# An attention and channel-mix kernel: w_v loaded in halves, a fused blend, w_k scaled in pieces, and a new instruction order

## The chip, the cores and the metric

The kernel runs on one core of a Trainium2 chip. The time is device time in microseconds (us). Most executions of the kernel before agree within 0.3%. A run more than 1.5% above the fastest of its own kernel is called slow. All traces cited are single executions; their span is some 1.8 us shorter than the time of the same run. A transfer is *issued* when an engine hands it to the DMA queues, and *lands* when its data have arrived.

## The reference

Linear attention for 8 batches of 8 heads, 576 positions of 64 channels, then an RMS norm, then an RWKV channel mix over 512 channels:

```python
kv  = einsum('bhsd,bhse->bhde', k, v)
out = einsum('bhsd,bhde->bhse', q, kv)
x   = out / sqrt(mean(out * out) + 1e-6) * g_norm        # heads side by side: 512 channels
xk  = mu_k * x + (1 - mu_k) * x_prev                     # x_prev: x one position earlier
xr  = mu_r * x + (1 - mu_r) * x_prev
k2  = relu(xk @ w_k) ** 2                                # 512 -> 1024
y   = sigmoid(xr @ w_r) * (k2 @ w_v)                     # 1024 -> 512
```

## The kernel before

The kernel is a list of some 580 named pieces and a hand-searched order of them. Each engine runs its own pieces in list order, so a list entry also fixes the order in which a DMA queue is fed. `kv3.0` is batch 3's k-v product, `qt3` the DMA transpose of its q, `ss5 rr5 ro5 rb5` the sum of squares, reciprocal root, store to and fetch from DRAM of batch 5's scales, `k0`, `r0`, `v0` the products with w_k, w_r and w_v of group 0 (512 rows), `store0.1` the output store of its second half. Nine groups cover the 4608 rows.

```python
def load_w(dst, s, due, land, name):
    def fn(_):
        nc.gpsimd.dma_start(out=dst, in_=s.rearrange("(c p) n -> p c n", p=128))
    return add({"POOL": 0.8}, fn, due=due, land=land, name=name)
# ... cut
p_wv = load_w(w_v_sb, moe_w_v, -698, 5.2, "w_v")        # one transfer
# ... cut: batches 3 to 7 turn q by DMA; the next batch's loads wait for that
def q_turn(_):
    nc.sync.dma_start_transpose(out=get(qT).rearrange("q i (j p) -> q (i j) p", j=NJ),
                                in_=q2.t.rearrange("p i j c -> p (i j c)"))
c = add({"SP": 3.1}, q_turn, deps=parts, ...)
gate = add({"POOL": 0.3}, lambda _: nc.gpsimd.tensor_copy(out=turned, in_=qT.t[0:1, 0, 0:1]), deps=[c], ...)
for n in ("k", "v", "q"):
    whole[(n, b + 1)].deps.append(gate)
# ... cut: batches 5 to 7 send their scales through DRAM
def rms_out(_):
    nc.sync.dma_start(out=get(rd), in_=rc.t[0:128:16, :])
def rms_back(_):
    for e in range(2):
        nc.gpsimd.dma_start(out=get(rs)[64 * e:64 * e + 64],
                          in_=rd.t.rearrange("(i e) c -> e i c", e=2)[e].partition_broadcast(64))
# ... cut: zeros that keep TensorE busy in known gaps ("idle:12" in the order)
def filler(n):
    i = 1 if k_seen[1] < NHP else 0
    for _ in range(n if k_seen[i] < NHP else 0):
        nc.tensor.matmul(get(k_ps[i])[:, 0, 0:128], zero[:, 0:128], zero[:, 128:256], start=not k_seen[i],
                         stop=not k_seen[i])
```

Of the kernel before, what the change touches and what calls it, by code (L numbers as in the profile page):

```python
# [898 lines left out]
```

## Time and profile before

| | before |
|---|---|
| time | 204.55 us median of 3 (204.27 to 204.92; a fourth run came with the result) |
| TensorE busy | 193.6 us of a span of 202.5 |
| VectorE, ScalarE | 147.4, 113.6 us |
| first w_k product, first w_v product | 17.74, 35.88 us in the chain |
| end of TensorE's work | 198.4 us |

The lines themselves are in the prediction below. For the comparison that follows, here are the entries of the two DMA-issuing engines in the kernel before that turned out to matter. First the sync engine's timeline; its columns are the start, how long the issue took, engine, source line, operation, out<-in, and count.

```profile
45.40 1.17 SPq L724 DMA_DIRECT2D out_dram<-out  x2
48.54 4.83 SPq L556 DMA_TRANSPOSE qT<-q  x1
53.43 12.49 SPq L724 DMA_DIRECT2D out_dram<-out  x10
```

One row tile of group 0 is stored (two issues, 256 KB), then batch 3's q is transposed, and only then come the other stores. Next, GpSimd's timeline around batch 7:

```profile
109.75 1.26 POOL L634 DMA_DIRECT2D rs<-rd  x2 [14.94 <-DVE out L821]
110.99 0.18 POOL L562 COPY turned<-qT 1x1 bf16<-1x1 bf16 x1
111.11 0.79 POOL L273 DMA_DIRECT2D q<-in_q_dram  x1
111.90 0.78 POOL L273 DMA_DIRECT2D k<-in_k_dram  x1
112.66 0.78 POOL L273 DMA_DIRECT2D v<-in_v_dram  x1
```

Batch 5's scales are fetched first, the gate opens, then q, k and v of batch 7 go out in 2.3 us. By their time to landing they arrive at 119.5, 122.4 and 125.5.

### The profile page before, as it was taken

Reading aid. Unit: us, or ns where it says so; the run is one execution under the profiler, and the core shown is the slowest. Engines: PE = TensorE matmul, PEld = TensorE weight load, DVE = VectorE, ACT = ScalarE, POOL = GpSimd, SP = SyncE. Lnnn points to the kernel's source line nnn. Section 1 sums busy time; section 2 is a strip of 40 time slices with the busy share of each in tenths; the row PEclk is TensorE's granted clock in tenths of the full one; section 3 lists DMA queues with packets and bytes.
Section 4 is the critical chain, followed back from the end, with each engine's and each line's share of the span. In section 5 each row is a group of like instructions: output and inputs, shape, how many; then the busy total and the mean of one; then the engine's idle time right before and its main releaser. Section 6 shows DMA issues by size and latency. Waiting matters only on the chain.

```text
span 202.5 us, 4076 instructions
## 1 busy us (share of the span) xinstructions
PE 193.6 (96%) x1625; PEld 102.9 (51%) x1645; DVE 147.4 (73%) x324; ACT 113.6 (56%) x145; POOL 32.6 (16%) x52
## 2 busy tenths in 40 slices
PE   7999699999999999999999999999999999999991
PEld 7767484454553444444447744444444444444451
...
DMA  6999999999999999998997999950360117000643
GB/s 166 201 204 204 206 204 206 204 203 227 223 174 189 213 148 128 203 203 191 211 172 151 230 195 196 204 190 3 65 209 2 47 38 228 0 0 0 182 130 107
DMA packets 39800, 31.69 MB, mean 156 GB/s; under 512 B 13636, under 2 KB 34916, under 8 KB 39780
## 3 DMA queue, kind: packets, MB, share of 16 engines
...
q1 hardware_dynamic: 17620, 12.42, 27.0%
q10 hardware_dynamic: 672, 0.89, 1.3%
...
HBM read 35.33 MB, written 9.46 MB: 221 GB/s over the span
## 4 chain that ended last, share of the span: by engine, by line
PE 88%; DVE 4%; DMA 2%; ACT 2%; issue 1%; SPq 0%; DVEq 0%
PE mm L743 28%; PE mm L817 27%; PE mm L795 16%; PE at L520 3%; PE at L599 3%; DMA out<-in_q_dram 2%; PE at L651 2%; PE mm L763 2%; PE at L834 2%; PE mm L834 2%; PE mm L476 2%; PE at L577 1%; ACT uT L184 1%; PE mm L713 1%; PE at L621 1%
## 5 line engine op out<-in xcount | busy, mean ns | idle before, releaser
L743 PE MATMUL mm<-xk,w_k 128*128 128x512 bf16 (+1 forms) x282 | 58.7, 355 | 0.4 <-issue 0.2
L817 PE MATMUL mm<-w_v,sqk 128*128 128x512 bf16 x249 | 57.7, 379 | 0.5 <-issue 0.2
L747 ACT ACTIVATE relu<-mm 128x1024 bf16<-128x1024 f32 x36 | 36.9, 1026 | 35.1 <-PE mm L743 30.7
L743 PEld LDWEIGHTS <-w_k 128*128 128x128 bf16 x288 | 27.3, 98 | 26.1 <-issue 1.6
L817 PEld LDWEIGHTS <-sqk 128*128 128x128 bf16 x256 | 24.5, 98 | 29.1 <-issue 0.9
L795 PE MATMUL mm<-w_r,xr 128*128 128x512 bf16 x137 | 33.7, 380 | 0.4
L750 DVE TENSOR_TENSOR sqk<-relu 128x1024 bf16<-128x1024 bf16 x32 | 21.5, 688 | 12.1 <-ACT relu L747 12.0
L821 DVE TENSOR_TENSOR out<-mm,sig 128x1024 f32<-128x1024 f32 x16 | 19.5, 1221 | 11.7 <-PE mm L817 11.6
L800 ACT ACTIVATE sig<-mm 128x1024 bf16<-128x1024 f32 x18 | 18.3, 1023 | 16.7 <-PE mm L795 16.5
L795 PEld LDWEIGHTS <-xr 128*128 128x128 bf16 x144 | 13.4, 98 | 15.8 <-issue 0.9
L193 ACT ACT_TABLE_LOAD x14 | 18.0, 1283 | 1.4 <-PEq L883 1.2
L693 DVE TENSOR_SCALAR md<-d,cols 128x576 bf16<-128x576 bf16 x56 | 18.1, 365 | 0.3
L184 ACT CAST uT<-at 128x576 bf16<-128x576 f32 x21 | 12.8, 643 | 7.1 <-PE at L599 6.9
L667 DVE TENSOR_TENSOR xT<-uT,rs 128x1152 bf16<-128x1152 bf16 x14 | 10.6, 755 | 5.3 <-ACT rs L655 5.3
L713 PE MATMUL mm<-zero 128*128 128x128 bf16 x131 | 12.2, 257 | 1.1 <-DVE zero L243 1.1
L606 DVE TENSOR_TENSOR sq<-uT 128x576 bf16<-128x576 bf16 x28 | 11.9, 453 | 0.6 <-ACT uT L184 0.3
L655 ACT ACTIVATE rs<-at,eps 128x576 bf16<-128x576 f32 x16 | 11.5, 740 | 0.9 <-PE at L651 0.7
L713 PEld LDWEIGHTS <-zero 128*128 128x128 bf16 x131 | 10.3, 119 | 2.2 <-DVE zero L243 1.1
L634 POOL DMA_DIRECT2D rs<-rd x6 | 3.7, 629 | 45.2 <-DVE md L693 17.5
L696 DVE TENSOR_TENSOR xk<-md,xT 128x1152 bf16<-128x1152 bf16 x14 | 10.6, 759 | 0.5
L696 DVE TENSOR_TENSOR xr<-md,xT 128x1152 bf16<-128x1152 bf16 x14 | 10.6, 758 | 0.5
L679 DVE TENSOR_TENSOR d<-xT 128x1152 bf16<-128x1152 bf16 x14 | 10.6, 755 | 0.3
...
## 6 DMA issues: line engine op xcount, KB each, us to landing
...
v<-in_v_dram POOLq DMA_DIRECT2D x6, 576.0 KB, 12.1
...
```

The costliest lines, as they stand in the source:

```text
L184: nc.scalar.copy(out=dst, in_=src)
L193: nc.scalar.preload_act_table_set(name)
L693: nc.vector.tensor_scalar(out=get(md)[:, hp], in0=d.t[:, hp], scalar1=cols[:, m0 + hp:m0 + hp + 1], scalar2=None, op0=ALU.mult)
L696: nc.vector.tensor_tensor(out=dst[:, hs, c0:c0 + S], in0=md.t[:, hs], in1=xT.t[:, hs, 0:S], op=ALU.add)
L713: nc.tensor.matmul(get(k_ps[i])[:, 0, 0:128], zero[:, 0:128], zero[:, 128:256], start=not k_seen[i], stop=not k_seen[i])
L743: nc.tensor.matmul(get(ps)[:, fc % 2, a0:a1], w_k_sb[:, cc, 128 * fc:128 * fc + 128], xk[:, cc, x0:x0 + a1 - a0], start=(cc == 0), stop=(c ...
L747: nc.scalar.activation(out=get(rt), in_=ps.t, func=AF.Relu)
L750: nc.vector.tensor_mul(out=get(sqk)[:, 2 * f2:2 * f2 + 2, :], in0=rt.t, in1=rt.t)
L795: nc.tensor.matmul(get(ps)[:, ci % 2, :], xr[:, cc, n0:n0 + 128], w_r_sb[:, cc, :], start=(cc == 0), stop=(cc == NHP - 1))
L800: nc.scalar.activation(out=get(sg), in_=ps.t, func=AF.Sigmoid)
L817: nc.tensor.matmul(get(ps)[:, ci % 2, :], sqk.t[:, fc, 128 * ci:128 * ci + 128], w_v_sb[:, fc, :], start=(fc == 0), stop=(fc == NFC - 1))
L821: nc.vector.tensor_mul(out=get(ot)[:, xs, :], in0=ps.t[:, xs, :], in1=sg.t[:, xs, :])
```

## The change

The intent: the first w_v products need not wait for the whole of w_v, the first blends are one VectorE instruction instead of two, the first w_k products need only a quarter of w_k scaled, and a new search of the order is to use this freedom. The whole order list is replaced. The diff of the code (dependency lists that only follow from it are cut):

```diff
-        p_wk.append(scale_w(w_k_sb[:, :, cs], l, None, f"g.w_k{i}", {"DVE": both["DVE"]}))
+        p_wk.append([scale_w(w_k_sb[:, c2:c2 + 2, cs], l, None, f"g.w_k{i}{c2}",
+                             {"DVE": dve_us(1024, 4), "ACT": act_us(1024, True, True)}) for c2 in (0, 2)])
...
-    p_wv = load_w(w_v_sb, moe_w_v, -698, 5.2, "w_v")
+    p_wv = [load_w(w_v_sb[:, 4 * i:4 * i + 4, :], moe_w_v[C * i:C * i + C, :], -698 + 0.1 * i, 2.6, f"w_v{i}")
+            for i in range(2)]
...
+            def fused(_, key, dst, m0):
+                nc.vector.scalar_tensor_tensor(out=dst[:, hp0, c0:c1], in0=d.t[:, hp0, c0:c1],
+                                               scalar=cols[:, m0 + hp0:m0 + hp0 + 1], in1=xT.t[:, hp0, c0:c1],
+                                               op0=ALU.mult, op1=ALU.add)
...
+                if n == 1 and key == "k":
+                    done.append(add({"DVE": dve_us(w) + 0.03}, lambda _, a=(key, dst, m0): fused(_, *a),
+                                    deps=[df, p_cols], bufs=[xT, d], name=f"x{key}0.{hp0}"))
+                    continue
```

The whole order list is replaced. Two places of it (cut to the entries concerned):

```diff
-... store0.0#2 qt3 store0.0 store0.1#2 ... store0.1 gate3 loadq4.0 ...
+... store0.0#2 ... store0.0 ... store0.1#2 store0.1 qt3 gate3 loadq4.0 ...
...
-... r3.2 ss5 r3.3 v3.2.0 ... rr5 ... kv6.0 ... ro5 ... rb5 ... gate6 loadq7.0 ... loadk7.0 loadv7.0 kv7.0 ...
+... v3.2.0 ... gate6 loadq7.0 store3.0 ss5 rr5 ro5 rb5 ... kv6.0 ... loadk7.0 loadv7.0 ... kv7.0 ...
```

More of the change, by code (lines that the diff above doesn't have):

```diff
@@ L15 @@
 ORDER = """
-setup ident loadq0.2 loadk0.2 first_k first_q cast_q:DVE cast_k:DVE first_v table cast_v:DVE idle:61 qtr0.0
-qc0.0#2:ACT idle:2 kv0.0 kvc0.0:ACT qtr0.1 qc0.1#2:ACT loadv0.2 idle:6 kv0.1 kvc0.1:ACT ident9 edge qc0.1:DVE
-qc0.0:DVE idle:1 u0.0 uc0.0:DVE sq0.0 small tr9 u0.1 u0.0#2 uc0.1:ACT sq0.1 cols loadv0.6 loadk0.6 loadq0.4
-uc0.0#2:ACT sq0.0#2 idle:5 ss0.0 rr0.0 mul0.0 idle:3 ss0.1 rr0.1 mul0.1 d0.0 mr0.0:DVE idle:1 ss0.0#2 rr0.0#2
-mul0.0#2 kv0.3 kvc0.3:DVE d0.1 qtr0.2 qc0.2#2:ACT d0.0#2 mk0.0:DVE xk0.0 loadq0.6 qtr0.3 qc0.3#2:ACT qc0.3:ACT
@@ L21 @@
-loadv0.4 qc0.2:ACT loadk0.4 idle:7 kv0.2 idle:4 u0.3 uc0.3:DVE sq0.3 kvc0.2:ACT u0.2#2 uc0.2#2:ACT u0.2 uc0.2:ACT
-sq0.2 idle:13 ss0.3 w_k0 g.w_k0 sq0.2#2 ss0.2 rr0.2 mul0.2 rr0.3 idle:8 ss0.2#2 rr0.2#2 d0.2 mul0.3 loadq1.0 k0.a0.0
-idle:6 qtr1.0 mk0.0#2:ACT qc1.0:ACT mk0.2:DVE mul0.2#2 mr0.1#2:DVE loadk1.0 mk0.1#2:ACT mk0.1:DVE xr0.0 xk0.2
-idle:14 k0.a0.2 loadv1.0 kv1.0 d0.2#2 xk0.1 k0.a0.1 mk0.2#2:DVE kvc1.0:ACT mr0.0#2:ACT u1.00 d0.3 mk0.3#2:DVE
-mk0.3:DVE xk0.3 xk0.2#2 xk0.0#2 xr0.0#2 w_k1 uc1.00:ACT sq1.00 u1.01 uc1.01:ACT sq1.01 g.w_k1 mr0.2:DVE mr0.2#2:DVE
@@ L26 @@
-k0.a0.3 relu0.00 mr0.3:ACT k0.b0 ss1.00 k0.a1.0 relu0.10 mr0.1:DVE ksq0.10 xr0.2 ss1.01 rr1.01 rr1.00 k0.a1.3
-k0.a1.1 k0.a1.2 relu0.01 mr0.3#2:ACT loadq1.4 w_r k0.b1 xr0.1 ksq0.00 xr0.3 loadv1.4 qtr1.2 loadk1.4 kv1.2 g.w_r:DVE
-xr0.2#2 r0.2 relu0.11 qc1.2:DVE kvc1.2:DVE u1.10 uc1.10:ACT r0.3 sig0.1 u1.11 r0.0 r0.1 sig0.0 ksq0.11 ksq0.01
-sq1.10 uc1.11:DVE sq1.11 ss1.11 ss1.10 rr1.10 mul1.0 d1.0 xk1.0 xr1.0 w_v v0.2.0 v0.2.1 v0.3.0 rr1.11 mul1.2 d1.2
-xk1.2 v0.3.1 out0.1 v0.0.0 v0.0.1 v0.1.0 loadk2.0 loadq2.0 qtr2.2 qtr2.0 v0.1.1 qc2.0:DVE out0.0 qc2.2:ACT k1.0
@@ L31 @@
-loadv2.0 kv2.0 kvc2.0:ACT k1.1 relu1.0 xr1.2 loadq3.0 ql3.3:DVE ql3.0:DVE ql3.1:DVE ql3.2:ACT loadk3.0 loadv3.0
-u2.10 uc2.10:DVE sq2.10 u2.01 uc2.01:ACT sq2.01 k1.2 k1.3 k1.4 u2.00 u2.11 store0.0#2 qt3 store0.0 store0.1#2
-relu1.1 uc2.11:DVE uc2.00:ACT sq2.00 ksq1.1 sq2.11 ksq1.0 k1.5 ss2.01 rr2.01 relu1.2 k1.6 ss2.10 rr2.10 store0.1
-gate3 loadq4.0 k1.7 relu1.3 ss2.00 rr2.00 mul2.0 r1.0 r1.1 sig1.0 r1.2 r1.3 ss2.11 sig1.1 loadv4.0 kv3.0 ksq1.2
-ksq1.3 v1.0.0 v1.0.1 v1.1.0 v1.1.1 d2.0 xk2.0 rr2.11 kvc3.0:ACT u3.11 uc3.11:ACT u3.10 uc3.10:ACT v1.2.0 v1.2.1
@@ L36 @@
-u3.01 u3.00 uc3.01:ACT v1.3.0 v1.3.1 mul2.2 d2.2 out1.0 xk2.2 ql4.1:ACT uc3.00:ACT ql4.3:DVE loadk4.0 store1.0#2
-store1.0 ql4.2:DVE ql4.0:DVE qt4 gate4 loadq5.0 out1.1 store1.1 k2.4 k2.5 relu2.2 sq3.00 sq3.10 xr2.2 sq3.01 sq3.11
-ksq2.2 xr2.0 k2.6 k2.7 relu2.3 ksq2.3 k2.2 ss3.10 rr3.10 k2.3 relu2.1 ss3.11 rr3.11 mul3.2 ss3.00 k2.0 rr3.00 d3.2
-k2.1 relu2.0 ss3.01 r2.0 rr3.01 mul3.0 ksq2.0 r2.1 sig2.0 kv4.0 r2.2 r2.3 kvc4.0:DVE ksq2.1 u4.10 u4.01 sig2.1
-uc4.01:ACT uc4.10:ACT v2.0.0 v2.0.1 v2.1.0 xk3.2 d3.0 sq4.01 xk3.0 sq4.10 u4.11 uc4.11:ACT u4.00 ql5.2:DVE
@@ L41 @@
-uc4.00:ACT ql5.1:ACT sq4.11 ql5.3:DVE ql5.0:DVE loadk5.0 loadv5.0 v2.2.0 v2.2.1 v2.1.1 out2.0 ss4.10 rr4.10 v2.3.0
-xr3.0 ss4.01 v2.3.1 out2.1 k3.4 k3.5 ss4.11 rr4.01 relu3.2 xr3.2 ksq3.2 k3.0 rr4.11 mul4.2 sq4.00 d4.2 xk4.2 k3.1
-relu3.0 ksq3.0 qt5 store1.1#2 store2.1#2 k3.6 k3.7 kv5.0 kvc5.0:ACT relu3.3 k3.2 u5.10 uc5.10:DVE u5.11 uc5.11:ACT
-ksq3.3 sq5.11 gate5 loadq6.0 k3.3 relu3.1 ksq3.1 u5.00 uc5.00:ACT sq5.00 u5.01 uc5.01:ACT r3.0 sq5.01 sq5.10 r3.1
-sig3.0 ss4.00 ql6.3:ACT ql6.1:DVE ql6.2:DVE ql6.0:DVE store2.0#2 store2.0 store2.1 v3.0.0 v3.0.1 v3.1.0 v3.1.1
@@ L46 @@
-out3.0 rr4.00 mul4.0 d4.0 xk4.0 r3.2 ss5 r3.3 v3.2.0 v3.2.1 v3.3.0 v3.3.1 rr5 xr4.2 sig3.1 out3.1 xr4.0 loadv6.0
-loadk6.0 kv6.0 k4.6 k4.7 relu4.3 k4.2 k4.3 kvc6.0:DVE qt6 u6.11 uc6.11:ACT ro5 relu4.1 store3.0 store3.0#2 u6.00
-uc6.00:DVE sq6.00 k4.0 u6.01 uc6.01:ACT u6.10 uc6.10:DVE ksq4.3 k4.1 relu4.0 k4.4 k4.5 relu4.2 r4.0 r4.1 sig4.0
-ksq4.1 ksq4.0 sq6.10 sq6.11 sq6.01 ss6 rr6 ro6 rb5 mul5.0 d5.0 gate6 loadq7.0 r4.2 ksq4.2 ql7.0:DVE ql7.3:DVE
-ql7.2:DVE ql7.1:DVE xk5.0 mul5.2 r4.3 sig4.1 v4.2.0 v4.2.1 v4.3.0 v4.3.1 d5.2 xk5.2 out4.1 v4.0.0 v4.0.1 v4.1.0
@@ L51 @@
-v4.1.1 loadk7.0 loadv7.0 kv7.0 out4.0 xr5.2 k5.4 k5.5 relu5.2 k5.6 k5.7 kvc7.0:DVE xr5.0 qt7 u7.10 u7.01 uc7.10:DVE
-uc7.01:ACT ksq5.2 rb6 mul6.2 sq7.10 k5.2 relu5.3 store3.1 store4.1#2 store3.1#2 store4.0 store4.1 u7.00 u7.11
-uc7.11:ACT uc7.00:ACT k5.3 relu5.1 k5.0 sq7.11 k5.1 relu5.0 r5.2 r5.3 sig5.1 r5.0 sq7.01 sq7.00 ss7 r5.1 sig5.0 d6.2
-ksq5.3 ksq5.1 rr7 mul6.0 ksq5.0 v5.2.0 v5.2.1 v5.3.0 v5.3.1 xk6.2 d6.0 xk6.0 k6.2 k6.3 relu6.1 out5.1 ro7 rb7 k6.0
-k6.1 relu6.0 xr6.0 k6.6 k6.7 relu6.3 ksq6.0 ksq6.3 ksq6.1 xr6.2 k6.4 k6.5 relu6.2 ksq6.2 v5.0.0 v5.0.1 v5.1.0 v5.1.1
@@ L56 @@
-out5.0 store5.1#2 store4.0#2 store5.1 r6.2 r6.3 v6.2.0 v6.2.1 sig6.1 v6.3.0 v6.3.1 mul7.2 mul7.0 d7.0 xk7.0 out6.1
-store6.1 d7.2 xr7.2 xk7.2 r6.0 r6.1 v6.0.0 v6.0.1 sig6.0 v6.1.0 v6.1.1 out6.0 store6.0#2 k7.4 k7.5 relu7.2 k8.6 k8.7
-k7.2 k7.3 relu8.3 xr7.0 ksq8.3 ksq7.2 relu7.1 ksq7.1 store5.0#2 store5.0 k7.6 k7.7 relu7.3 ksq7.3 store6.1#2
-store6.0 k7.0 k7.1 relu7.0 k8.0 k8.1 relu8.0 k8.2 k8.3 relu8.1 ksq7.0 r7.2 r7.3 v7.2.0 v7.2.1 ksq8.1 sig7.1 v7.3.0
-v7.3.1 out7.1 r7.0 r7.1 v7.0.0 v7.0.1 v7.1.0 v7.1.1 sig7.0 out7.0 store7.0#2 store7.1 store7.1#2 k8.4 k8.5 relu8.2
@@ L61 @@
-r8.2 r8.3 sig8.1 ksq8.2 ksq8.0 r8.0 r8.1 sig8.0 v8.0.0 v8.0.1 v8.1.0 v8.1.1 store7.0 out8.0 store8.0 out8.0#2
-store8.0#2 v8.2.0 v8.2.1 v8.3.0 out8.1 store8.1 v8.3.1 v8.3.0#2 v8.3.1#2 out8.1#2 store8.1#2 out8.1#3 store8.1#3
+setup ident loadq0.2 first_q first_k cast_k:DVE edge ident9 cast_q:DVE small idle:64 tr9 first_v cast_v:DVE qtr0.0
+qc0.0#2:ACT qc0.0:DVE cols idle:4 kv0.0 qtr0.1 loadk0.2 loadv0.2 idle:1 kv0.1 kvc0.1:DVE kvc0.0:ACT u0.0 qc0.1#2:ACT
+idle:3 u0.0#2 uc0.0#2:DVE sq0.0#2 qc0.1:ACT u0.1 uc0.0:ACT sq0.0 uc0.1:DVE sq0.1 loadv0.4 loadq0.4 loadk0.4 idle:4
@@ new lines @@
+qtr0.2 qc0.2#2:DVE idle:3 kv0.2 table ss0.0#2 idle:2 ss0.0 rr0.0#2 rr0.0 qc0.2:DVE kvc0.2:DVE mul0.0 d0.0 loadq0.6
+idle:6 ss0.1 rr0.1 qtr0.3 qc0.3:DVE loadk0.6 loadv0.6 idle:2 kv0.3 kvc0.3:ACT u0.2 mul0.1 qc0.3#2:DVE xk0.0
+mr0.0:ACT idle:3 u0.3 idle:2 u0.2#2 uc0.2:ACT uc0.3:ACT d0.1 sq0.2 w_k0 idle:7 ss0.2 xk0.1 sq0.3 idle:3 ss0.3
+uc0.2#2:ACT g.w_k00:ACT idle:10 k0.a0.0 rr0.3 mul0.0#2 d0.0#2 mr0.0#2:DVE sq0.2#2 mr0.1#2:DVE mul0.3 d0.3 rr0.2
+k0.a0.1 ss0.2#2 rr0.2#2 w_k1 g.w_k12:ACT mr0.3:ACT mk0.1:ACT g.w_k10:DVE idle:12 k0.a1.0 loadq1.0 k0.a1.1 qtr1.0
@@ new lines @@
+qc1.0:ACT loadv1.0 mul0.2 xk0.3 d0.2 mk0.0:ACT g.w_k02:DVE k0.a0.3 mul0.2#2 xk0.2 d0.2#2 mr0.2:DVE mk0.2:DVE
+mr0.1:DVE k0.a0.2 relu0.00 mk0.3:DVE mr0.3#2:DVE xk0.0#2 loadk1.0 k0.a1.2 k0.a1.3 kv1.0 kvc1.0:ACT u1.00 uc1.00:ACT
+mr0.2#2:ACT u1.01 relu0.01 xk0.2#2 xr0.0#2 k0.b1 relu0.11 ksq0.00 uc1.01:DVE sq1.01 ss1.01 sq1.00 ss1.00 rr1.00
+rr1.01 k0.b0 relu0.10 xr0.1 loadk1.4 w_r xr0.0 xr0.3 xr0.2#2 g.w_r:DVE xr0.2 r0.0 ksq0.11 ksq0.01 mul1.0 loadq1.4
+qtr1.2 qc1.2:DVE loadv1.4 kv1.2 kvc1.2:DVE r0.1 sig0.0 ksq0.10 u1.10 u1.11 r0.2 r0.3 sig0.1 uc1.10:DVE sq1.10 ss1.10
@@ new lines @@
+rr1.10 w_v0 v0.0.0 uc1.11:DVE sq1.11 ss1.11 d1.0 v0.2.0 xk1.0 xr1.0 w_v1 v0.0.1 v0.1.0 v0.1.1 v0.2.1 v0.3.0 rr1.11
+mul1.2 d1.2 xk1.2 out0.0 xr1.2 store0.0#2 loadq2.0 qtr2.0 qc2.0:ACT qtr2.2 v0.3.1 out0.1 qc2.2:DVE k1.2 k1.3 relu1.1
+ksq1.1 loadk2.0 loadv2.0 kv2.0 kvc2.0:ACT loadq3.0 ql3.1:ACT ql3.0:DVE ql3.2:DVE ql3.3:DVE k1.6 k1.7 u2.10
+uc2.10:ACT u2.11 relu1.3 store0.0 k1.0 k1.1 u2.01 uc2.11:DVE uc2.01:DVE sq2.01 u2.00 uc2.00:ACT relu1.0 sq2.00 k1.4
+k1.5 relu1.2 ksq1.2 ss2.01 rr2.01 r1.2 ss2.00 rr2.00 r1.3 sig1.1 r1.0 r1.1 sig1.0 sq2.11 loadk3.0 loadv3.0 kv3.0
@@ new lines @@
+ss2.11 rr2.11 mul2.0 ksq1.3 ksq1.0 v1.0.0 v1.0.1 d2.0 sq2.10 kvc3.0:DVE xk2.0 ss2.10 rr2.10 mul2.2 store0.1#2
+store0.1 qt3 gate3 loadq4.0 v1.1.0 v1.1.1 out1.0 d2.2 xk2.2 u3.11 uc3.11:ACT u3.01 uc3.01:ACT sq3.01 ql4.1:ACT
+ql4.3:ACT ql4.2:DVE ql4.0:DVE v1.2.0 v1.2.1 u3.10 uc3.10:ACT u3.00 v1.3.0 v1.3.1 out1.1 uc3.00:DVE sq3.11 sq3.00
+k2.0 k2.1 ss3.01 rr3.01 relu2.0 k2.2 k2.3 relu2.1 store1.0 ss3.11 ss3.00 rr3.00 rr3.11 k2.6 k2.7 relu2.3 xr2.2 xr2.0
+ksq2.1 ksq2.0 sq3.10 loadk4.0 mul3.0 ksq2.3 k2.4 k2.5 relu2.2 r2.0 ss3.10 loadv4.0 kv4.0 ksq2.2 r2.1 d3.0 xk3.0
@@ new lines @@
+kvc4.0:ACT rr3.10 mul3.2 d3.2 xk3.2 qt4 store1.0#2 v2.0.0 v2.0.1 v2.1.0 v2.1.1 gate4 loadq5.0 sig2.0 out2.0 u4.01
+uc4.01:ACT u4.10 uc4.10:ACT sq4.10 r2.2 loadv5.0 loadk5.0 ql5.2:DVE r2.3 sig2.1 ql5.0:DVE ql5.1:DVE ql5.3:ACT qt5
+store1.1#2 k3.6 u4.11 uc4.11:DVE u4.00 k3.7 uc4.00:DVE relu3.3 store2.0#2 gate5 xr3.2 sq4.00 k3.0 k3.1 relu3.0
+ss4.10 sq4.01 rr4.10 k3.4 k3.5 xr3.0 ss4.01 rr4.01 relu3.2 v2.2.0 v2.2.1 ksq3.3 ss4.00 sq4.11 store1.1 ss4.11 v2.3.0
+v2.3.1 out2.1 store2.1#2 rr4.11 mul4.2 ksq3.2 rr4.00 d4.2 r3.2 r3.3 sig3.1 k3.2 kv5.0 kvc5.0:DVE xk4.2 ksq3.0 k3.3
@@ new lines @@
+relu3.1 ksq3.1 store2.0 u5.01 uc5.01:ACT sq5.01 xr4.2 u5.10 uc5.10:ACT loadq6.0 ql6.3:DVE ql6.1:DVE ql6.0:DVE
+loadv6.0 loadk6.0 r3.0 r3.1 u5.11 uc5.11:ACT u5.00 uc5.00:ACT mul4.0 sq5.00 ql6.2:ACT qt6 v3.0.0 v3.0.1 v3.1.0
+v3.1.1 sig3.0 v3.2.0 v3.2.1 v3.3.0 v3.3.1 sq5.10 d4.0 xk4.0 sq5.11 out3.0 store3.0#2 gate6 loadq7.0 store3.0 ss5 rr5
+ro5 rb5 out3.1 store2.1 kv6.0 kvc6.0:DVE k4.4 k4.5 relu4.2 ksq4.2 xr4.0 k4.6 k4.7 relu4.3 k4.2 u6.01 uc6.01:ACT
+u6.11 uc6.11:DVE k4.3 relu4.1 k4.0 k4.1 u6.00 ksq4.1 uc6.00:DVE u6.10 sq6.11 uc6.10:ACT sq6.10 sq6.00 relu4.0 sq6.01
@@ new lines @@
+r4.2 r4.3 sig4.1 ksq4.3 ql7.3:DVE ksq4.0 ql7.0:ACT ql7.1:DVE ql7.2:ACT mul5.0 mul5.2 d5.0 d5.2 xk5.0 xk5.2 store3.1
+r4.0 ss6 r4.1 v4.0.0 sig4.0 v4.0.1 v4.1.0 v4.2.0 v4.2.1 v4.3.0 v4.1.1 out4.0 v4.3.1 out4.1 loadk7.0 loadv7.0 xr5.2
+qt7 store3.1#2 kv7.0 kvc7.0:DVE rr6 ro6 k5.4 k5.5 relu5.2 k5.2 k5.3 relu5.1 store4.0 store4.1#2 store4.0#2 xr5.0
+u7.00 u7.11 ksq5.2 uc7.00:DVE uc7.11:ACT sq7.11 k5.6 k5.7 relu5.3 sq7.00 ksq5.3 ksq5.1 k5.0 k5.1 relu5.0 ksq5.0 rb6
+mul6.0 mul6.2 u7.10 uc7.10:ACT u7.01 uc7.01:ACT d6.2 sq7.01 sq7.10 r5.0 r5.1 v5.0.0 v5.0.1 v5.1.0 v5.1.1 sig5.0
@@ new lines @@
+out5.0 ss7 rr7 ro7 r5.2 r5.3 v5.2.0 v5.2.1 v5.3.0 v5.3.1 sig5.1 d6.0 xk6.2 xk6.0 k6.6 out5.1 store5.1 store5.0 k6.7
+relu6.3 ksq6.3 k6.2 k6.3 relu6.1 k6.0 k6.1 relu6.0 k6.4 k6.5 relu6.2 rb7 xr6.2 xr6.0 r6.0 r6.1 ksq6.0 sig6.0 ksq6.1
+mul7.0 ksq6.2 store5.1#2 store5.0#2 store4.1 mul7.2 d7.0 d7.2 xk7.0 xk7.2 r6.2 r6.3 sig6.1 v6.2.0 v6.2.1 v6.3.0
+v6.3.1 out6.1 v6.0.0 v6.0.1 v6.1.0 v6.1.1 out6.0 store6.0#2 store6.1#2 store6.0 store6.1 k7.2 k7.3 relu7.1 k8.2 k8.3
+relu8.1 k7.6 k7.7 relu7.3 xr7.0 ksq7.1 xr7.2 ksq7.3 ksq8.1 k7.4 k7.5 relu7.2 k7.0 k7.1 relu7.0 ksq7.0 ksq7.2 k8.4
@@ L63 @@
+k8.5 relu8.2 k8.6 k8.7 relu8.3 k8.0 k8.1 relu8.0 ksq8.0 r7.2 r7.3 sig7.1 ksq8.3 r7.0 r7.1 v7.0.0 v7.0.1 v7.1.0
+sig7.0 v7.1.1 v7.2.0 v7.2.1 v7.3.0 v7.3.1 out7.0 store7.0#2 ksq8.2 out7.1 store7.1#2 store7.0 r8.2 r8.3 sig8.1 r8.0
+r8.1 sig8.0 v8.0.0 v8.0.1 out8.0 store8.0 v8.2.0 v8.2.1 out8.1 store8.1 v8.1.0 v8.1.1 v8.3.0 v8.3.1 v8.3.0#2
+v8.3.1#2 store7.1 out8.0#2 store8.0#2 out8.1#2 store8.1#2 out8.1#3 store8.1#3
 """.split()
@@ L479, in k_part @@
                                          stop=(k_seen[i] == NHP and fc % 2 == 1))
-                k_parts[i].append(add({"PE": 0.44}, k_part, deps=[ka, p_wk[i]], bufs=[k_ps[i]], mode="full",
+                k_parts[i].append(add({"PE": 0.44}, k_part, deps=[ka, p_wk[i][hp // 2]], bufs=[k_ps[i]], mode="full",
                                       due=T0 + 0.44 * (hp + NHP * i), name=f"k0.a{i}.{hp}"))
@@ L771, in mix @@
                     m = k_parts[i] if half == 0 else [add(
-                        {"PE": 1.75}, k_half, deps=need["k"] + [p_wk[i]], bufs=[ps], due=u, mode="full", name=f"k0.b{i}")]
+                        {"PE": 1.75}, k_half, deps=need["k"] + p_wk[i], bufs=[ps], due=u, mode="full", name=f"k0.b{i}")]
                     k_all += m
@@ L782, in mix @@
                 ms.append(add({"PE": 0.865}, lambda _, fc=2 * f2 + x, ps=ps: k_mm(_, fc, ps),
-                              deps=ms or need["k"] + [p_wk[f2 // 2]], bufs=[ps, sqk], due=u + x, mode="full",
+                              deps=ms or need["k"] + p_wk[f2 // 2], bufs=[ps, sqk], due=u + x, mode="full",
                               name=f"k{g}.{2 * f2 + x}"))
@@ L836, in mix @@
                             ms.append(add({"PE": 0.865 * (cs[1] - cs[0]) / C}, v_last,
-                                          deps=ms[-1:] or sqs + [p_wv, sg_done.deps[0]], bufs=[ps, sqk, ot],
+                                          deps=(ms[-1:] or sqs + [sg_done.deps[0]]) + [p_wv[part_]], bufs=[ps, sqk, ot],
                                           due=u + 2 * x + part_, mode="full", name=f"v{g}.{2 * c2 + x}.{part_}"))
@@ L851, in mix @@
                                   lambda _, ci=2 * c2 + x, part_=part_, ps=ps: v_mm(_, ci, part_, ps),
-                                  deps=ms[-1:] or sqs + [p_wv, sg_done.deps[0]], bufs=[ps, sqk, ot],
+                                  deps=(ms[-1:] or sqs + [sg_done.deps[0]]) + [p_wv[part_]], bufs=[ps, sqk, ot],
                                   due=u + 2 * x + part_, mode="full", name=f"v{g}.{2 * c2 + x}.{part_}"))
```

## The prediction

> **What bounds the kernel now.** I first read the page's busy table and slices, to see which engine is full and where it is not.
>
> ```profile
> PE 193.6 (96%) x1625; PEld 102.9 (51%) x1645; DVE 147.4 (73%) x324; ACT 113.6 (56%) x145; POOL 32.6 (16%) x52
> PE   7999699999999999999999999999999999999991
> DMA  6999999999999999998997999950360117000643
> ```
>
> TensorE is full from the third slice to the last but one. But "busy" counts filler: at L713 the kernel multiplies zeros to fill gaps, 131 times. So next I read the stretches between landmarks of the chain (columns: stretch, its length, PE, PEld, DVE, ACT, POOL busy, clock, DMA share, GB/s).
>
> ```profile
> 17.74:35.88 18.14, 16.52 (x221) 11.69 (x220) 15.51 (x46) 14.01 (x21) 5.53 (x7) 1.00 1.27 205
> 35.88:58.18 22.30, 21.88 (x245) 11.20 (x248) 18.70 (x39) 15.29 (x19) 2.66 (x4) 1.00 1.24 214
> 160.35:182.79 22.44, 22.34 (x103) 10.17 (x104) 10.81 (x18) 9.21 (x9) 0.00 (x0) 1.00 0.24 71
> 198.40:202.50 4.10, 0.00 (x0) 0.00 (x0) 0.75 (x2) 0.00 (x0) 0.00 (x0) 0.84 0.47 130
> ```
>
> From 35.88 us to 198.40 TensorE idles 1.3 us in all (0.42 in the first of these rows, about 0.1 in each of the others). No order of the same matmuls can win more than that there. The room is in the head, before 35.88, which the chain of work that ended last shows in order of time (start, us, what).
>
> ```profile
> 17.74 0.44 PE mm L476 x4
> 18.18 0.34 PE mm L713 x6
> ...
> 19.14 0.89 PE mm L713 x14
> ...
> 22.06 1.18 ACT uT L184 x2
> 23.24 0.94 ACT relu L747
> 24.18 0.04 issue
> 24.22 1.91 PE mm L763 x16
> ...
> 35.88 4.96 PE mm L817 x23
> ```
>
> The first real w_k product starts at 17.74, and the first w_v product at 35.88. Between them the chain leaves TensorE for two uT copies and a relu on ScalarE (22.06 to 24.22, less the end of the last matmul: about 1.5 us idle) and spends 0.34 + 0.89 us on fillers. So about 2.8 us can be won after 17.74, and more only if 17.74 itself moves.
>
> The second limit of the head is the load stream. From the timeline, with each transfer's issue-to-landing time:
>
> ```profile
> 8.14 0.79 POOL L304 DMA_DIRECT2D w_k<-in_moe_w_k_dram  x1
> 10.88 0.80 POOL L304 DMA_DIRECT2D w_k<-in_moe_w_k_dram  x1
> 12.29 0.81 POOL L304 DMA_DIRECT2D w_r<-in_moe_w_r_dram  x1
> 17.85 0.89 POOL L304 DMA_DIRECT2D w_v<-in_moe_w_v_dram  x1 [0.52 <-DMA q<-in_q_dram]
> ```
>
> With 8.0, 12.1, 14.7 and 17.2 us to landing, they land at 16.1, 23.0, 27.0 and 35.05. From 27.0 to 35.05 the stream brings w_v (1024 KB) and two half batches (288 KB each): 1600 KB in 8.05 us, 199 KB per us. It works off transfers in issue order, so a landing is a sum of sizes. w_v, whole, lands 0.8 us before its first use: the first v piece could not have come earlier than 35.05 however fast the rest was.
>
> **What the skill says.** (1) "VectorE: DVE Perf Modes", section "The perf-mode tier table": tensor_scalar in bf16 reaches 4x, tensor_tensor 2x; scalar_tensor_tensor, which the fused xk is, has no row. The trace agrees on large tiles: 128x2048 tensor_scalar 748 ns (w_r), 128x1152 tensor_tensor 755 ns. The fused form's speed no run shows yet. (2) "DMA: Bandwidth & Descriptors", "Issuing engines are not separate DMA queues": transfers of all engines share 16 engines and interleave. The slices agree: about 200 GB/s throughout the head. (3) "ScalarE: Activation LUTs", "What ACT_TABLE_LOAD costs": about 1283 ns each; the trace has 14 of mean 1283 ns. (4) "TensorE: Matmul & The Clock Gate", "What's actually happening": a cold array runs at half clock. The first 61 fillers took 6.21 us, 102 ns each; six later ones 0.34 us, 57 ns each. So I price later fillers at 57 ns.
>
> **The change, part by part.**
> *w_v in halves.* One more issue on POOL (0.8 us, off the path). The first 512 KB lands 512/199 = 2.6 us sooner, at 32.5; the second at 35.05. The new order puts v0.0.0 and v0.2.0 (0.86 us each) before the first use of the second half, so v may start at 33.3 with no wait. This allows up to 35.88 - 33.3 = 2.6 us; it gives only what the rest of the head delivers.
>
> *xk fused for 256 columns, four times.* It removes a tensor_scalar and a tensor_tensor. Their mean durations are 311 and 291 ns, but back to back each costs about 0.20 us (successive starts 19.51, 19.71, 19.91). One operation at one element per cycle would be (an estimate, from the 0.96 GHz that the same page states) 256/960 = 0.27 us plus 0.07: 0.34. Saved: 4 x (0.40 - 0.34), about 0.2 us of VectorE, and one md less before each xk.
>
> *w_k scaled in four.* VectorE had 2 x 2048 columns (0.66 and about 0.95 us by successive starts). It keeps two pieces of 1024 (about 0.35 each) and ScalarE takes two, about 1.1 us each: 256 and 320 columns took 519 and 560 ns, 0.64 ns per column, so 1024 take about 1.0. That frees 0.9 us on VectorE and adds 2.1 to ScalarE. The first product no longer waits for a scale of all four head pairs.
>
> *Order.* w_k's second half is now issued before batch 1's loads and lands at 16.1 + 2.6 = 18.7 instead of 23.0, so its products can fill the hole at 22.06. Fillers fall from 131 to 126. VectorE up to the second group-0 output takes on more copies (two more 576-column uT casts, 0.8 each; more qT), net about +1.2 us; it has 1.8 us idle near 24 to 27 and more near 9 to pay with. ScalarE gets one more table load (15): its first copy brings one load, the rsqrt set is loaded after it; by my walk it has 0.4 us spare. The later transposes of q move ahead of output stores, and the gated loads with them: slack, not time.
>
> *The head walked by hand* with the durations above. The q cast is now behind the k cast and ident9, so v's cast ends near 8.15 instead of 7.93 and kv0.0 starts 0.4 late; but the first u no longer waits for a second qT copy (about 9.5 instead of 9.77). First rsqrt near 12.5 instead of 11.6. ScalarE scales w_k's first piece from about 16.35 to 17.4, so k0.a0.0 starts near 17.5, only 0.3 sooner. Then: twelve fillers to 19.3, a1.0 and a1.1 to 20.25, qtr1.0 to 20.8, a0.3, a0.2, a1.2, a1.3 to 22.6, a wait for batch 1's k (16.1 + 2.6 + 2.6 + 3 x 1.45 = 23.1 by the stream) and kv1.0 to 23.7, relu and kv copy to 24.1, u1 to 24.55, b1 to 26.3, ss1 and b0 to 28.55, r0.0 and qtr1.2 to 30.0, kv1.2, r0.1, u1 to 31.85, r0.2, r0.3, ss1.10 to 33.85. So v0 starts at 33.85 with the same work done but one ss1.11 (0.25): 35.88 - 33.85 - 0.25 = 1.8 us won, if no handover costs anything. The walk counts few semaphore delays over some forty hops, so I take 1.4 of it.
>
> After v0: kv2.0 needs batch 2's v, landed at 43.7 before; by the walk kv2.0 starts at 43.9, just behind it. The relay of batch 3's q waits for its landing at 46.7 as before. I take 0.1 us of net loss in the 162 us that follow. Sum: 204.55 - 1.4 + 0.1 = 203.2, rounded down a little for the looser gates.
>
> **Rivals.**
> *A: the load stream decides.* The bytes before batch 2's v and batch 3's q are the same, so their landings cannot move, and an early store of group 0 would even delay them. For: the DMA row is at 9 tenths throughout the head. Against: the walk shows these two just met. Then TensorE waits near kv2.0 and gain shrinks to 0 to 0.7: 203.9 to 204.5.
> *B: VectorE becomes the bound between 28 and 48.* It runs without a gap there before and has 1.2 us more to do. Then relu, sqk and out come late and mm buffers hold TensorE: 203.8 to 205.
> *C: the head gains all and the later waits go too:* 1.8 + the w_v cap's remainder 0.7 + part of the 1.3 us: 201.5 to 202.
> *D: the q relays, earlier in program order for batch 6, block VectorE or ScalarE until q lands.* Before, q6 landed at 100.9, 8.4 us after issue. Costs 0.5 to 1.5 us near 92 to 98.
>
> **Range and chances.** Half way between the walk and its losses: 203.1 us, with 201.7 to 204.6 holding C's better half and most of A, B, D. More than 2% faster means below 200.5, which needs over 4 us: more than the holes of the head and all later idle together (2.8 + 1.3) unless 17.74 moves by far; 0.03. Slower by 2% needs 4 us of new waits: 0.02.
>
> **What would show it.** Right: first w_k product within 0.5 us of 17.5; no ScalarE step in the chain near 22 to 24; w_v halves landing near 32.5 and 35; first w_v product near 34; TensorE idle after it still 1 to 2 us. Fused xk near 0.34 us by successive starts. Wrong: a DMA wait before kv1.0 or kv2.0 over 0.5 us, sqk or out releases of TensorE (B), TensorE gaps behind q relays near 92 to 98 (D), or a first w_k product later than 18.2.

## More of the kernel before

The two facts that matter later: the sync engine (SP) issues output stores, q transposes and the scale stores in one sequence, and GpSimd (POOL) issues all casting loads and the scale fetches in another. An entry that waits holds up everything behind it in its sequence (the fetch that waits 6.72 us in the profile after is an example).

## The result and the profile after

| | before | after |
|---|---|---|
| time, median (range) | 204.43 us (204.27 to 204.92, 4 runs) | 211.38 us (209.71 to 212.83, 4 runs) |
| ratio of fast runs | | 1.0333, interval 1.0255 to 1.0412 |
| mean granted TensorE clock | 0.997 (profiled run) | 0.980 to 0.988 |

All these runs are fast ones. The ratios here and below compare the fast runs of the two kernels; they are not quite the ratios of the medians. The kernel became 3.3% slower. The profiled run of the changed kernel is the slowest of its four (212.83 us).

The page after, with TensorE's busy share, its slices, its clock and the DMA share:

```profile
PE 195.6 (93%) x1618; PEld 103.6 (49%) x1640; DVE 148.3 (70%) x325; ACT 115.3 (55%) x143; POOL 33.0 (16%) x53
PE   7999899999499999999999992899999999999992
PEclk9999999999999999999999999589999999999999
DMA  6999999999949969989999799930057006000445
```

There are two new dents in TensorE's row, one in the eleventh slice (about 53 to 58 us) and one in the twenty-fifth (about 127 to 132), and behind the second the clock row falls to 5. TensorE's timeline names what ended these two gaps (in brackets the idle time and its releaser), and shows that the head did what was hoped:

```profile
33.97 1.03 PE L828 MATMUL mm<-w_v,sqk 128*128 128x512 bf16 x4
...
58.07 0.95 PE L531 MATMUL at<-v,k 96*64 96x64 bf16 x48 [2.73 <-DMA v<-in_v_dram]
...
132.39 1.49 PE L531 MATMUL at<-v,k 96*64 96x64 bf16 x48 [4.30 <-DMA v<-in_v_dram]
```

The first w_v product starts at 33.97 (the timeline of the kernel before has it at 35.71). But batch 3's k-v product waits 2.73 us for v and batch 7's waits 4.30 us. The stretches around the second wait (start and end, length, PE, PEld, DVE, ACT, POOL busy, clock, DMA share, GB/s):

```profile
55.34:58.07 2.73, 0.00 (x2) 0.03 (x2) 1.58 (x3) 2.71 (x3) 0.00 (x0) 1.00 1.31 103
128.09:132.39 4.30, 0.00 (x1) 0.03 (x2) 3.32 (x5) 0.00 (x0) 0.00 (x0) 0.94 1.25 88
132.39:139.84 7.45, 7.23 (x67) 3.51 (x71) 2.43 (x5) 1.02 (x1) 1.26 (x2) 0.58 0.93 251
139.84:206.90 67.06, 66.73 (x330) 30.63 (x336) 38.16 (x67) 29.73 (x30) 1.23 (x2) 1.00 0.24 67
```

After the second wait the clock is at 0.58 for 7.45 us, which alone costs about 7.45 x 0.42 = 3.1 us. The starts agree: from batch 7's k-v product to the end of TensorE's work it is 74.50 us here and 71.55 before, so 2.95 us more for the same work. After the first, shorter wait the clock stays at 1.00.

Why the loads were late is in the two issuing engines. The sync engine after:

```profile
42.16 4.31 SPq L735 DMA_DIRECT2D out_dram<-out  x8
48.19 6.91 SPq L567 DMA_TRANSPOSE qT<-q  x1
```

All four row tiles of group 0 (eight issues, 1 MB) now go out before batch 3's transpose, in the middle of the loads of batch 3's k and v. Those landed at 49.5 and 53.3 before; they land at 53.7 and 57.9 now, and their last part shares the DMA engines with the transpose (as the old kernel's v did). And GpSimd after, around batch 7:

```profile
109.68 0.77 POOL L273 DMA_DIRECT2D q<-in_q_dram  x1 [0.39 <-DVE kv L186]
117.17 1.26 POOL L645 DMA_DIRECT2D rs<-rd  x2 [6.72 <-DMA rd<-rc]
118.53 0.79 POOL L273 DMA_DIRECT2D k<-in_k_dram  x1
119.31 0.78 POOL L273 DMA_DIRECT2D v<-in_v_dram  x1
```

The fetch of batch 5's scales stands between q's load and those of k and v, and waits 6.72 us for the scales to arrive in DRAM. So k and v are issued at 118.5 and 119.3 instead of 111.9 and 112.7, and v lands at 132.3 instead of 125.5.

TensorE's own clock of progress (starts in the timelines, us) sums it up:

| | before | after | after, behind (+) or ahead (-) |
|---|---|---|---|
| first w_v product | 35.71 | 33.97 | -1.7 (one ss of 0.25 still to do: -1.5) |
| batch 3's k-v product | 57.24 | 58.07 | +0.8 (two ss of 0.25 each still to do: +1.3) |
| batch 7's k-v product | 126.80 | 132.39 | +5.6 |
| end of TensorE's work | 198.35 | 206.89 | +8.5 |

(`ss` is a sum of squares; the new order puts some behind the product.) The parts add up: -1.5 + 2.73 + 4.30 + 2.95 for the lowered clock is 8.5. The medians differ by less, 7.0 us, since the profiled run is the slowest.

### The profile page after: what moved, and what is told of

Read it like the earlier page. It is cut to its first block, busy times and chain, and to the rows that moved or that the text cites. A ratio compares the mean times of both kernels' runs of the same rounds, so it can differ in the third digit from the quotient of the medians.

```text
span 211.1 us, 4070 instructions
## 1 busy us (share of the span) xinstructions
PE 195.6 (93%) x1618; PEld 103.6 (49%) x1640; DVE 148.3 (70%) x325; ACT 115.3 (55%) x143; POOL 33.0 (16%) x53
## 4 chain that ended last, share of the span: by engine, by line
PE 63%; DMA 27%; POOL 6%; issue 2%; DVE 1%; ACT 0%; DVEq 0%; ACTq 0%
PE mm L754 22%; PE mm L828 20%; DMA v<-in_v_dram 19%; PE mm L806 10%; DMA k<-in_k_dram 5%; PE at L531 3%; DMA rd<-rc 3%; POOL q L273 2%; PE mm L774 2%; POOL k L273 2%; PE at L845 2%; PE mm L845 2%; PE at L610 2%; PE at L662 1%; POOL v L273 1%
## 5 line engine op out<-in xcount | busy, mean ns | idle before, releaser
L754 PE MATMUL mm<-xk,w_k 128*128 128x512 bf16 (+1 forms) x281 | 60.0, 364 | 0.6 <-issue 0.4
L754 PEld LDWEIGHTS <-w_k 128*128 128x128 bf16 x288 | 28.1, 100 | 28.0 <-issue 4.3
L806 PE MATMUL mm<-w_r,xr 128*128 128x512 bf16 x135 | 33.0, 380 | 0.6 <-issue 0.3
L531 PE MATMUL at<-v,k 96*64 96x64 bf16 x336 | 7.4, 203 | 7.5 <-DMA v<-in_v_dram 7.0
L184 ACT CAST uT<-at 128x576 bf16<-128x576 f32 x17 | 10.3, 640 | 4.7 <-PE at L610 4.4
L724 PE MATMUL mm<-zero 128*128 128x128 bf16 x126 | 11.7, 251 | 1.1 <-DVE eps L244 1.1
L531 PEld LDWEIGHTS <-k 96*64 96x64 bf16 x336 | 6.6, 118 | 10.1 <-issue 9.4
L573 POOL COPY turned<-qT 1x1 bf16<-1x1 bf16 x4 | 0.7, 176 | 67.2 <-DMA qT<-q 67.2
```

Of the source, the lines that this page charges most:

```text
L531: nc.tensor.matmul(get(ps)[64 * r:64 * r + 64, 0, c:c + HD], kin.t[:, 2 * hp + e, HD * j:HD * j + HD], vin.t[:, 2 * hp + e, HD * j:HD * j ...
L754: nc.tensor.matmul(get(ps)[:, fc % 2, a0:a1], w_k_sb[:, cc, 128 * fc:128 * fc + 128], xk[:, cc, x0:x0 + a1 - a0], start=(cc == 0), stop=(c ...
L806: nc.tensor.matmul(get(ps)[:, ci % 2, :], xr[:, cc, n0:n0 + 128], w_r_sb[:, cc, :], start=(cc == 0), stop=(cc == NHP - 1))
```

## The experiments

**Theory Q**: the order in which the two issuing engines feed the DMA queues costs the time, at two places, and the second wait costs again through the clock. **Rival W**: the new parts and the copies moved to VectorE and ScalarE cost it.

### e6_old_order: the parts without the new order

The change's code, with the order list of before (w_v0 w_v1 for w_v, four scalings on VectorE for two, no separate md, the product of mu and the difference, for the fused columns).

> The parts of the change (w_v in halves, fused xk, w_k scaled in four pieces, all four on VectorE) in the order of the kernel before. Theory Q (the loss lies in the new order): the same as the kernel before within 0.6 us, 203.8 to 205 us. Rival W (the parts cost): 206 us or more.

Measured: 204.22 us median (204.03 to 205.51, 20 runs), ratio 0.9988, interval 0.9975 to 1.0001. The parts alone cost nothing and win nothing; the first w_v product starts at 36.24. The loss lies in the order. W falls as far as it blames the parts; the copies that it also blames are part of the new order, and e4 and e7 bear on them.

### e4_head_only: the new head, then the old order

All the parts and the new order up to `out0.1`, then the old order for all pieces that are left.

> All parts of the change and its order up to the second output of group 0, then the order of the kernel before for all that is left. Theory Q: the head's 1.9 us are kept and none of the new waits comes, 202.3 to 203.5 us. Rival W (what the new head moves to VectorE and ScalarE is given back later): 204.5 or more.

Measured: 203.91 us (203.49 to 204.52, 4 runs), ratio 0.9979, interval 0.9956 to 1.0002. So the new head does no harm later, but 202.3 to 203.5 was expected: 0.5 us by the medians is all that stays, and the interval reaches no gain at all. The first w_v product starts at 34.15, and then:

```profile
44.09 0.95 PE L530 MATMUL at<-v,k 96*64 96x64 bf16 x48 [0.51 <-DMA v<-in_v_dram]
```

TensorE, being ahead, runs into batch 2's v, which lands at 43.9 here and landed at 43.7 before. It starts batch 3's k-v product 0.5 us before the old kernel (56.70 to 57.24), batch 6's also 0.5 (106.37 to 106.91), and ends 0.7 us before it (197.69 to 198.35). What is lost of the lead is lost before batch 3's product; the old order keeps the rest. This is the prediction's rival A, with its wait near `kv2.0` and its 203.9 to 204.5 us.

### e1_kv7_loads: batch 7's k and v ahead of the scale fetch

```diff
-loadq7.0 store3.0 ss5 rr5 ro5 rb5 ... loadk7.0 loadv7.0 xr5.2 qt7
+loadq7.0 loadk7.0 loadv7.0 store3.0 ss5 rr5 ro5 rb5 ... xr5.2 qt7
```

> The changed kernel, with the loads of batch 7's k and v moved ahead of the store and fetch of batch 5's scales on GpSimd, directly behind the load of batch 7's q. Theory Q (queue order costs the time): the two loads are issued near 111 us instead of 118.5, v of batch 7 lands before about 126, TensorE no longer waits 4.3 us for it near 128 and its clock is not lowered after it (2.7 us more), so 5 to 7 us less than the changed kernel: 204.5 to 206.5 us. Rival W (the extra work of the new parts and of the moved copies on VectorE and ScalarE is what costs): nothing changes, 210 to 212.

Measured: 212.71 us (212.03 to 214.13, 4 runs), ratio 1.0416. My expectation missed. Batch 7's v lands at 124.6 and its product no longer waits, but:

```profile
127.20 0.95 PE L530 MATMUL at<-v,k 96*64 96x64 bf16 x48
133.91 0.58 PE L753 MATMUL mm<-xk,w_k 128*128 128x512 bf16 x1 [5.77 <-DVE out L831]
```

The next product waits 5.77 us for VectorE to empty a PSUM buffer (the memory that TensorE's products go to). VectorE's timeline says what held that up:

```profile
126.92 0.76 DVE L677 TENSOR_TENSOR xT<-uT,rs 128x1152 bf16<-128x1152 bf16 x1 [6.67 <-DMA rs<-rd]
...
132.65 2.35 DVE L831 TENSOR_TENSOR out<-mm,sig 128x1024 f32<-128x1024 f32 x2
```

VectorE stood 6.67 us before batch 5's scales, whose two halves now landed behind k and v at 125.6 and 126.8 instead of 121.0 and 121.9, and the outputs stand behind that multiplication in its order. Putting one transfer first only exchanged the waiting engine. The place of `rb5` in GpSimd's sequence was a symptom; the scales themselves come too late.

### e2_qt3_first: the transpose ahead of the stores

```diff
-ql3.3:DVE ... store0.0 ... store0.1#2 store0.1 qt3 gate3
+ql3.3:DVE qt3 ... store0.0 ... store0.1#2 store0.1 gate3
```

> The changed kernel, with the transpose of batch 3's q put ahead of three of group 0's four stores on the sync queue, as the kernel before had it. Theory Q: k and v of batch 3 land near 49.5 and 53.5 instead of 53.7 and 58.0, the 2.7 us wait of TensorE at 55.4 goes. The stores now delay batch 4's loads instead, which have some slack. The second wait, near 128, stays in part: 1 to 3 us less than the changed kernel, 208.5 to 210.5 us. Rival W: no change.

Measured: 202.87, 204.65, 208.13 and 208.21 us, all below the range expected. Two of these count as slow, so the ratio of the fast runs, 0.9969 (0.9916 to 1.0022), rests on two runs and says little. The trace is of a slow run, 208.21; the two fast ones left none, so whether they wait at batch 7 too is not known. What it shows of batch 3 is clear: v lands at 53.5, its product starts at 56.07 without a wait (before 57.24, after 58.07). Batch 7's still waits 2.89 us in this run. In the two long runs the mean clock is 0.990 and 0.982, in the two short ones 1.000 and 0.999. In the profiled one it is 0.70 and 0.87 in the two 4 us stretches after the wait (some 1.7 us lost). The first collision is shown, with its cause.

### e3_both: both moves

The edits of the two runs before, together.

> The changed kernel with both moves of the two runs before. Theory Q: both waits gone, the 1.9 us won in the head stay: 202.3 to 204 us, faster than the kernel before by 0.4 to 2 us. Rival W: 209 to 211.

Measured: 210.72 us (209.89 to 212.02, 4 runs), ratio 1.0317. Also a miss, for the reason of e1: batch 3's product starts at 55.60 without a wait, but a w_k product waits 5.13 us at 131.62 for the output behind batch 5's scales.

### e5_warm_wait: keeping TensorE busy in the wait

```diff
             def kv_mm(_, hps=hps, hp0=hp0, ps=ps):
+                for _i in range(70 if b == 7 else 0):
+                    nc.tensor.matmul(get(ps)[:, 0, 0:128], zero[:, 0:128], zero[:, 128:256], start=True, stop=True)
```

> The changed kernel with 70 more products of zeros (about 4 us at 57 ns each) just ahead of batch 7's k-v product, so that TensorE is kept busy in most of the wait for batch 7's v. Theory C (the wait costs twice: 4.3 us itself, and some 2.7 us because the clock is lowered after it): the wait stays, the granted clock stays at 0.99 or more, 2 to 3.5 us less than the changed kernel, 208 to 209.5 us. Rival: the lower clock has another cause than the idle time, the records show it again and the time is 211 or more.

Measured: 209.00 us (208.34 to 210.01, 4 runs), ratio 1.0228, mean clock 0.998 to 1.000, against 211.38 with 0.980 to 0.988 for the changed kernel: 2.4 us less by the medians, from work that computes nothing. The wait is still there, filled:

```profile
126.88 4.07 PE L527 MATMUL at<-zero 128*128 128x128 bf16 x70
131.07 0.95 PE L532 MATMUL at<-v,k 96*64 96x64 bf16 x48
```

```profile
131.07:138.50 7.43, 7.38 (x84) 3.67 (x85) 4.19 (x9) 3.20 (x4) 1.26 (x2) 1.00 0.96 245
```

In the same 7.4 us after batch 7's v the clock is 1.00, not 0.58. From batch 7's product to the end of TensorE's work it is 71.56 us, as in the kernel before (71.55) and not the 74.50 of the changed kernel. So the second wait is paid for twice, and the second payment, 2.9 us, is the clock's.

### e7_qt3_norm5 and e8_norm5: batch 5's scales early

Theory Q2: the scales come late because the new order puts `ss5` behind all of group 3's w_v products and its store (`ro5`) behind two output stores on the sync engine. In e8 this alone is undone, with `rb5` ahead of batch 7's loads again; in e7 the transpose move of e2 is added.

```diff
-sig3.0 v3.2.0 v3.2.1 v3.3.0 v3.3.1 sq5.10 d4.0 xk4.0 sq5.11 out3.0 store3.0#2 gate6 loadq7.0 store3.0 ss5 rr5 ro5 rb5
+sig3.0 sq5.10 sq5.11 ss5 rr5 ro5 v3.2.0 v3.2.1 v3.3.0 v3.3.1 d4.0 xk4.0 out3.0 store3.0#2 rb5 gate6 loadq7.0 store3.0
```

> Only the second of the two moves: batch 5's scales early, group 0's stores still ahead of batch 3's transpose. Theory Q2: the 2.7 us wait for batch 3's v near 55 stays, the one near 128 goes with its lowered clock: 204.8 to 206.5 us. If the first collision alone carried on into the second one: 208 or more.

> The changed kernel with the transpose of batch 3's q ahead of group 0's stores, and with batch 5's sum of squares, rsqrt, store and fetch of its scales moved before the second half of group 3's w_v products, so that the scales are fetched before batch 7's q, k and v, as in the kernel before. Theory Q2 (the new order brings batch 5's scales too late, so that their fetch and batch 7's loads collide, whichever goes first): the fetch is issued near 108 instead of 115 to 117, v of batch 7 lands before 125, no wait over 0.5 us at batch 7's k-v product nor for the group-4 output, clock 0.99 or more, 202.3 to 203.6 us. Rival (the transfers of this stretch are too many for any order of theirs): a wait of 2 us or more stays near 125 to 132, 205 us or more.

Measured, e8: 206.43 us (205.54 to 207.79, 4 runs), ratio 1.0112, as expected: the scales are fetched at 108.9, v of batch 7 lands at 125.8, there is no wait at batch 7's product and the clock of the profiled run is 0.998. At batch 3's product TensorE still stands 1.72 us; the profile puts that wait down to a sigmoid, but v of batch 3 lands at 56.9 and the product starts at 57.02.

Measured, e7: 204.51 us (203.57 to 205.56, 14 runs), ratio 0.9999, interval 0.9977 to 1.0020. Both collisions are gone, and with them the whole loss of 7 us. The products of batches 3 and 7 start without a wait:

```profile
56.42 0.95 PE L530 MATMUL at<-v,k 96*64 96x64 bf16 x48
...
127.94 0.95 PE L530 MATMUL at<-v,k 96*64 96x64 bf16 x48
```

So Q2 holds. But 204.5 is the time of the kernel before, not the 202.3 to 203.6 that I expected: part of that miss is the next run.

### e7b_again: a second look at e7

> The kernel with both moves once more, for a second profile: the first one showed a 1.7 us wait for the scaling of w_k's second half near 19 to 20.6, which landed late. If that is jitter of the load stream, this profile has a wait of 0.5 us or less there and ends near 203.6 us; if the wait belongs to this order, it is there again and the time is 204.5 or more.

Measured: 204.09 us, one run. In the first profile of e7 the second half of w_k's scaling had come late and TensorE waited 1.71 us for it at 20.62; here there is no such wait, and the first w_v product starts at 33.69. So that wait is not in every execution, and the new head has no slack against it. But the time is 204.09 and not 203.6. TensorE is 2.0 us ahead of the old kernel at batch 3's k-v product (55.20; 1.5 if the two ss still to do are counted), 1.0 at batch 6's (105.91 to 106.91), 0.3 at batch 7's (126.49 to 126.80) and at the end (198.05). The first loss is the repair's own. With the same TensorE work, batch 5's product to batch 6's is 11.79 us in the changed kernel and 12.41 here: `ss5`, moved forward, now waits between its eight small matmuls for VectorE's squares and takes 0.88 us to the next piece instead of 0.36. The second loss is this:

```profile
119.48 7.08 PE L827 MATMUL mm<-w_v,sqk 128*128 128x512 bf16 x31 [0.66 <-DVE sqk L760]
```

VectorE's timeline has, just ahead of that squaring, a copy of batch 7's q that waited 0.84 us for its load:

```profile
118.40 0.42 DVE L185 COPY q<-q 96x384 bf16<-96x384 bf16 x2 [0.84 <-DMA q<-in_q_dram]
118.74 0.68 DVE L760 TENSOR_TENSOR sqk<-relu 128x1024 bf16<-128x1024 bf16 x1
```

This is the prediction's rival D, at batch 7 instead of batch 6.

### e9_before_stores: one of the collisions alone, in the kernel before

```diff
-store0.0#2 qt3 store0.0 store0.1#2 ... store0.1 gate3
+store0.0#2 store0.0 store0.1#2 ... store0.1 qt3 gate3
```

> The kernel before with one thing alone from the new order: all four stores of group 0 ahead of batch 3's transpose on the sync queue. Theory Q: k and v of batch 3 land some 4 us later, v near 57.5, a little after TensorE wants it at 57.2, and all gated loads after it move by as much: 204.8 to 206.5 us. If nothing is lost (204.2 to 204.7), the stores cost the changed kernel only because it was ahead there.

Measured: 205.08 us (204.26 to 210.38, 20 runs, one of them slow), ratio 1.0037, interval 1.0017 to 1.0058. The total fits, the place does not. In the profiled run (206.38 us) v of batch 3 lands at 55.1, in time for 57.84. The delay is passed from gate to gate (batch 4's q is issued at 59.1 instead of 56.0) and comes out at batch 6:

```profile
109.18 0.95 PE L520 MATMUL at<-v,k 96*64 96x64 bf16 x48 [1.27 <-DMA k<-in_k_dram]
```

So the stores cost the old kernel 0.8 us by the medians; most of the 2.73 us in the changed kernel came because its v landed 2.8 us later still and TensorE was ahead. Its stores also went out earlier (from 42.2, here from 46.0) and delayed k as well (53.7, here 49.5).

### e10_head_kv2: e4 with batch 2's product one piece later

e4 with `kv2.0` behind `k1.1` instead of ahead of it, so that batch 2's v is there.

> The hybrid of the new head and the old remainder, with batch 2's k-v product put one piece (k1.1, 0.86 us) later, since TensorE stood 0.5 us before it waiting for v of batch 2. If the load stream caps the head's gain only at this product: 0.3 to 0.5 us less than the hybrid, 203.3 to 203.7 us, the best of all. If the gain is given back elsewhere: 203.8 to 204.3.

Measured: 203.91 us (203.47 to 204.06, 6 runs), ratio 0.9966, interval 0.9938 to 0.9994: the only interval that lies wholly below the kernel before, by a third of a per cent. But the median is that of e4, 203.91, so the move itself is not shown to win anything. The wait for v is gone and batch 2's product starts at 44.43, but TensorE then waits 0.47 us, until 45.85, for the copy of that product instead: the time is in the range that was expected if the gain is given back elsewhere.

## Why the prediction was wrong

**What bounds the kernel, and the head: right.** The first w_k product started at 17.25 (17.5 in the walk), batch 1's k-v product waited for k until 23.08 (23.1), the halves of w_v landed at 32.4 and 34.9 (32.5 and 35.05), and v began at 33.97 (33.85). As a start time the walk was closer than the discount that I gave it. But its 1.8 us were counted from the chain's 35.88; from the timeline's 35.71 the gain measured is 1.5. One reading was careless: TensorE's row is not full from the third slice on, its fifth is at 6 tenths, which is the hole that the chain then shows at 22 to 24 us.

**The parts: small and partly mis-sized.** The fused blend takes 478 ns alone and 0.40 us by successive starts (19.12 to 19.52 in e7b), not 0.34, so it saves nothing against two operations of 0.20. A w_k piece on ScalarE takes 1142 ns (1.0 to 1.1 was estimated). Neither e6 (all four w_k pieces on VectorE) nor e4 (two on ScalarE) shows a loss from it.

**The step that failed** is "The later transposes of q move ahead of output stores, and the gated loads with them: slack, not time", with its sum, "I take 0.1 us of net loss in the 162 us that follow". I compared TensorE's and VectorE's orders of the two kernels carefully and the issuing engines' hardly. Batch 3's transpose moved behind three more row tiles of stores, and batch 5's scales moved into the middle of batch 7's loads; both were in the orders that I had. In place of 0.1 us the runs show 2.73 us of wait at batch 3, 4.30 us at batch 7 and 2.95 us of lowered clock.

**Rival A** named the stream and an early store, but only as a limit on the gain. With the old order behind the new head it came true (e4: 0.51 us before `kv2.0`, 203.91 us). Its bound of 204.5 us took for granted that a delayed load costs at most what the head had won. **Rival B** did not happen. **Rival D** is there, at batch 7, once the collisions are removed: TensorE stands 0.66 us.

**The chance of "slower", 0.02,** rested on "Slower by 2% needs 4 us of new waits". The number was fair, and two loads were enough to make them. I had also left out that a wait can lower the clock, although I had used the skill's page on it to price the fillers.

**Why nothing of the head's 1.5 us is left even in e7** is seen in two traces, at single places. In e4 it goes before batch 3's product, 0.51 us of it at the wait for batch 2's v. In e7b it lasts until batch 5's product; then `ss5`, where the repair put it, costs 0.6 us, and the squaring behind the copy of batch 7's q 0.7. That a still better order would keep the 1.5 us is not shown: no run removed both of these.

## What to carry to other kernels

When an order is changed, compare the sequences of the engines that issue DMAs as closely as those of the compute engines: for each entry ask what it waits for and which loads stand behind it. A kernel whose TensorE is 96% busy can still have loads that land just in time (batch 6's k landed at 106.8 before, 0.1 us ahead of its use), and such loads set the pace as soon as anything else gets faster. A wait of a few microseconds on TensorE may cost well over half as much again through the clock (2.95 us after the wait of 4.30); filler matmuls in that wait won back 2.4 us.

## What the Trainium skill lacked or had wrong

- "VectorE: DVE Perf Modes", "The perf-mode tier table", has no row for scalar_tensor_tensor. Here a 128x256 bf16 one takes 478 ns, and 0.40 us back to back, against 0.20 each for a tensor_scalar and a tensor_tensor of the same size.
- "TensorE: Matmul & The Clock Gate", "What's actually happening", has the clock at half after at least one idle window of about 3.4 us, at full after one busy window, and calls the windows free-running. The rise agrees: in the changed kernel, e1, e2 and e3 the lowered clock is 0.50 for one or two stretches of 3.41 us (131.88 to 138.71 in the changed kernel) and rises at the end of the first that had 3.34 us of TensorE work or more; 2.68 us were not enough. The fall needs no idle window. With the 13 traces cut into stretches of 3.41 us, counted from the recorded changes of the clock, the full clock fell after every stretch with 1.58 us of TensorE work or less and after none with 1.62 or more. So a wait of 2.89 us could lower it (e2, 1.58 us of work in the stretch) and one of 2.73 us not (the changed kernel at batch 3, where the wait lay across two stretches with 1.92 and 2.07).
- "DMA: Bandwidth & Descriptors", "DMA Transpose (X-bar)", does not say what a plain load gets beside a transpose. Here the engines moved 103 GB/s and 88 GB/s in the two waits, with a transpose under way and the DMA share as high as ever, against about 200 GB/s in the head.
- The same page's "Issuing engines are not separate DMA queues" says that several issuing engines only save issue time. In this kernel the issuing engine decided more: a fetch that waited 6.72 us on GpSimd held up two loads that were free to go. I found no page that spells out what a waiting issue does to the loads behind it.
